# Attention gradient on one core: the queries for dK by copies and DMA transposes from SBUF instead of by a round trip through DRAM

## The chip, the cores and the metric

The kernel runs on one core of a Trainium2 chip. The metric is the device time in microseconds (us) of that core, the median over several executions. The engines of the core are TensorE (PE in the profile, its weight loads PEld), VectorE (DVE), ScalarE (ACT), GpSimd (POOL) and SyncE (SP), which only issues transfers. Transfers run on 16 DMA engines.

## The reference, cut to what matters

The program computes two blocks side by side, and for both the output and all gradients (out_0 to out_8). Block A is linear attention. Block B, in which the change lies, is attention with 16 query heads of 28 columns and one shared key and value head, over 2048 positions:

```python
q = (x @ wq).reshape(B, S, H, Dh).transpose(0, 2, 1, 3)   # H = 16, Dh = 28, S = 2048
k = x @ wk                                                # one head
v = x @ wv
scores = jnp.einsum("bhqd,bkd->bhqk", q, k) * (Dh ** -0.5)
p = softmax(scores)
o = jnp.einsum("bhqk,bkd->bhqd", p, v)
out = o.transpose(0, 2, 1, 3).reshape(B, S, H * Dh) @ wo
...
_out, _vjp = jax.vjp(f, A_x, A_wqkv, ..., B_wo)
_grads = _vjp(grad_out)
```

The gradient with respect to the scores, dS, is needed twice: dQ = dS k, and dK = dS^T q summed over all heads. dK is what the changed operand is for: its matmuls need q with query positions on the partitions.

## The kernel before, in words

Phase A (up to L527, about the first 195 us) does linear attention and its gradients. `phase_B_pre` (L529) projects x to q, k and v of block B. The queries lie in the tile R1, shape 128 x 4 x 2048: the partition is a column of a head (four heads of 32 rows each, 28 of them used), the second index is the group of four heads, the third is the query position. Row 0 of each 32 carries a shift that keeps the exponential in range. `q_shift` (L608) computes it for 512 positions, and `put_shift` (L615) writes it into R1 with four small transfers from GpSimd's queue.

The loop from L894 ("the core") runs over steps `u`, 512 of them and a tail of 28. Eight steps make a block `b`: one chunk of 256 query positions (`qc`, eight chunks), for one pair of heads (eight pairs). A step handles two tiles of 128 keys. The order of the work in the loop is written out by hand (`manual_schedule`), so each engine takes its instructions in the order in which the loop emits them. Work on one tile is spread over many steps:

- step u: TensorE forms scores (`rows_SD`, L668), ScalarE takes the exponential of both halves (L914, L964) into eT. After every fourth step SyncE transposes that group of eT to eN with a DMA transpose of 1 MB (L966).
- step u + 16: TensorE forms dP. VectorE multiplies one half by eT (L925). ScalarE copies the other half to cp (L927), and GpSimd multiplies it by eT (L928). The two products are dsT. The pool of dsT has five buffers, that of cp three.
- step u + 18: VectorE transposes dsT in squares of 32 to dsx (L995).
- from step u + 19: dQ (`dq_mm`); at odd steps dK (`dk_m`, L834), with dsx as one operand and qX as the other, first at u = 27. dV (`dv_mm`, L869) needs eN and the normalised output gradient don; the first at u = 20 needs the first two transposes of eT, the next at u = 28 the two after these.
- once a block: `o_norm` (L798) at steps with u mod 8 = 2, with three operations on GpSimd (prod L808, don L811, R L812); `row_D` (L814) at 4, with one on GpSimd (L817); then TensorE transposes don (L825) at 6. The queries of a finished block are overwritten with dQ (L949).
- in steps 1 to 25, odd ones, `do_proj` (L876) adds four matmuls of 512 columns and a copy on VectorE (L886).

qX for a chunk has the query positions of one partition group on its partitions, 32 for each a in 0 to 3, and for each position all 512 rows of heads. So the same q stands in four places, once for each row group of TensorE that `dk_m` uses. In the kernel before it is made so:

- for positions 0 to 1023, `phase_B_pre` transposes R1 with four DMA transposes (L598) into a tile that lies in gaT, and SyncE stores that as 1 MB in DRAM, the scratch qn_d (L599);
- for positions 1024 to 2047, four DMA transposes ahead of the loop (L893) write a tile qn that lies in one of the two qX buffers; GpSimd stores it in four parts in the steps 34, 42, 50 and 58 (L930);
- each qX is read from qn_d with four transfers of 256 KB from GpSimd's queue (L937): for chunk 0 in steps 10, 14, 18 and 22, for chunk 1 in 66 to 78, for chunk qc from 2 on in four steps of the 64 before, at u mod 64 = 34, 42, 50 and 58.

GpSimd also loads wo for the output projection in step 86 (L940). Transfers with GpSimd as issuer use queue 0, those of SyncE queue 1.

Of the kernel before, what the change touches and what calls it, by code (L numbers as in the profile page):

```python
# [11 lines left out]
BF16 = mybir.dt.bfloat16  # L12
# [13 lines left out]
def kernel(  # L26
# [40 lines left out]
    R2 = R2x[:, 1:NS + 1, :]  # L67
    R3 = reg.tile([P, 4, 1408], BF16, name="R3")
    R4 = reg.tile([P, 4, 512], BF16, name="R4")
    qn_d = dpool.tile([S, 512], BF16, name="qn_d")  # L70
    wqT_d = dpool.tile([512, D], BF16, name="wqT_d")
    wkvT_d = dpool.tile([64, D], BF16, name="wkvT_d")
    wo_d = dpool.tile([512, 512], BF16, name="wo_d")
# [51 lines left out]
    def phase_A(pa, cA, cB, awk, psA):  # L125
# [398 lines left out]
                nc.gpsimd.dma_start(wkvT_d[32 * w:32 * w + 32, 3 * P:D], wt[0:32, 4 * w + 3, 64:128])  # L524
        for q4 in range(4):
            dma_T(v4(R2), xa, 4 * q4, 4)
        return xbT, wq_pad, rep, bsel, gaB[:, 0:8, :], ga[:, 8:12, :], [flat(gaB[:, 2 * i + 8:2 * i + 10, :]).bitcast(F32) for i in range(3)]  # L527

    def phase_B_pre(pa, cA, awk, psA, io):  # L529
        xbT, wq_pad, rep, bsel, qn, sh, tmp = io  # L530
        kT, vT, vaug, kn, qT = kT_rep, vT_rep, vaug_, kn_, R1

        def gen(shape, dt=F32):
            return psA.tile(shape, dt, name="agen")

        ones16 = cA.tile([P, H], BF16, name="ones16")
        nc.gpsimd.memset(ones16[:], 1.0)
        nc.gpsimd.memset(ones16[0:1, :], 0.0)
        neg = cA.tile([P, 1], F32, name="neg")
        nc.gpsimd.memset(neg[:], 0.0)  # L540
        for j in range(4):
            nc.gpsimd.memset(neg[32 * j:32 * j + 1, :], -1.0)
        sel = cA.tile([P, 32], BF16, name="sel")
        nc.gpsimd.tensor_copy(out=sel[:], in_=identB[:, 0:32])
        nc.gpsimd.memset(sel[0:1, :], 0.0)
        kmx = cA.tile([H, NQC], F32, name="kmx")
        sqk = []
        def k_max(qc, sq):
            ps = gen([H, 512])
            mm(ps[:, :], ones16[0:32, :], sq[0:32, :])  # L550
            nc.vector.tensor_reduce(out=kmx[:, qc:qc + 1], in_=ps[:, :], axis=AX.X, op=ALU.max)

        prev = None
        for qc in range(NQC):
            for w, dst in [(0, kT), (1, vT)]:
                ps = gen([P, 512])
                for c in range(4):
                    mm(ps[:, :], rep[:, w, c, :], xbT[:, c, qc * 512:(qc + 1) * 512], start=(c == 0), stop=(c == 3))

                if w:  # L560
                    nc.vector.tensor_scalar(out=dst[:, qc * 512:(qc + 1) * 512], in0=ps[:, :], scalar1=neg[:, 0:1],
                                            scalar2=None, op0=ALU.add)
                else:
                    nc.scalar.activation(out=dst[:, qc * 512:(qc + 1) * 512], in_=ps[:, :], func=ACT.Identity,
                                         bias=neg[:, 0:1])
            sq = awk.tile([P, 512], BF16, name="osb")
            nc.vector.tensor_tensor(out=sq[0:32, :], in0=kT[0:32, qc * 512:(qc + 1) * 512],
                                    in1=kT[0:32, qc * 512:(qc + 1) * 512], op=ALU.mult)
            if prev is not None:
                k_max(qc - 1, prev)  # L570
            prev = sq
        shifts = [flat(sh)[0:H, i * 512:(i + 1) * 512] for i in range(2)] + [flat(R3)[r:r + H, 5120:5632] for r in (32, 0)]
        for qc in range(NQC):
            qs = slice(qc * 512, (qc + 1) * 512)
            pn = psA.tile([P, 512], F32, name="aacc")
            sqs = []
            for g in range(6):
                if qc == 0 and g == 2:
                    k_max(NQC - 1, prev)
                    nc.vector.tensor_reduce(out=kmax2[:], in_=kmx[:], axis=AX.X, op=ALU.max)  # L580
                if g < 4:
                    ps = gen([P, 512])
                    for c in range(4):
                        mm(ps[:, :], wq_pad[:, c, g * P:(g + 1) * P], xbT[:, c, qs], start=(c == 0), stop=(c == 3))
                    nc.scalar.activation(out=qT[:, g, qs], in_=ps[:, :], func=ACT.Copy)
                    sq = awk.tile([P, 512], BF16, name="osb")
                    nc.vector.tensor_tensor(out=sq[:, :], in0=qT[:, g, qs], in1=qT[:, g, qs], op=ALU.mult)
                    sqs.append(sq)
                if g >= 2:
                    mm(pn[:, :], bsel[:, g - 2, :], sqs[g - 2][:, :], start=(g == 2), stop=(g == 5))  # L590
            if qc == NQC - 1:
                break
            q_shift(pn, shifts[qc], tmp)
            if qc < 2:
                put_shift(shifts[qc], qs)
            if qc == 1:
                for g in range(4):
                    nc.sync.dma_start_transpose(qn[:, :, g * P:(g + 1) * P], qT[:, g, 0:1024])  # L598
                nc.sync.dma_start(qn_d[0:1024, :].rearrange("(t p) c -> p t c", p=P), qn)  # L599
        for rows, dst in [(vT, vaug_), (kT, kn_)]:  # L600
            ps = gen([P, NS, 32])
            for st in range(NS):
                mm(ps[:, st, :], rows[:, st * P:(st + 1) * P], sel[:, :])
            nc.vector.tensor_copy(out=dst, in_=ps[:])
        nc.gpsimd.memset(vaug_[:, :, 0:1], 1.0)
        return pn, shifts
# [5 lines left out]
        nc.vector.tensor_scalar(out=a.bitcast(i32), in0=a.bitcast(i32), scalar1=1, scalar2=None, op0=ALU.logical_shift_right)  # L612
        nc.vector.tensor_scalar(out=shift, in0=a, scalar1=1.004 * 2.0 ** 63.5, scalar2=None, op0=ALU.mult)

    def put_shift(shift, qs):  # L615
        for g in range(4):
            nc.gpsimd.dma_start(R1[:, g, qs].rearrange("(j r) s -> j r s", r=32)[:, 0, :], shift[4 * g:4 * g + 4, :])

    R3f = flat(R3)
    kT_rep, vT_rep = R3f[:, 0:2048], R3f[:, 2048:4096]  # L620
# [15 lines left out]
    with ExitStack() as cs_:  # L636
# [54 lines left out]

        woTp, gbT = R4, R2.rearrange("p t (c k) -> p t c k", k=P)

        identF = pp_.tile([P, P], F32, name="identF", bufs=1)
        make_identity(nc, identF[:])
        oTs = pp_.tile([P, 256], F32, name="oTs", bufs=1)
# [132 lines left out]
        def don_copy(b):  # L829
            r = 64 * (1 - b % 2)  # L830
            doT[b] = pw_.tile([P, 256], BF16, name="doT", bufs=2)
            nc.vector.tensor_copy(out=doT[b][r:r + 64, :], in_=tps2.pop(b)[r:r + 64, 0:256])

        def dk_m(b, m):  # L834
            qc, pair, g, hp = blk(b)
            h, B, s = m // 8, (m // 2) % 4, m % 2
# [51 lines left out]
        do_slots = {2 * i + 1: (i, 0, 512) for i in range(13)}  # L888
        do_slots.update({32 + 8 * n: (13 + n // 4, n % 4 * P, n % 4 * P + P) for n in range(12)})
        with tc.manual_schedule():  # L890
            qn = pqa_.tile([P, 8, 512], BF16, name="qX")
            for g in range(4):
                nc.sync.dma_start_transpose(qn[:, :, g * P:(g + 1) * P], R1[:, g, 1024:2048])  # L893
            for u in range(NU + 28):  # L894
                w = u - 16
                hasS = u < NU
# [18 lines left out]
                if u == 1:  # L915
                    q_shift(pn3, shifts[3], [pd_.tile([P, 2, 512], BF16, name="dsT").rearrange("p a b -> p (a b)").bitcast(F32)
                                             for _ in range(1)])
                    for qc in (2, 3):
                        put_shift(shifts[qc], slice(qc * 512, qc * 512 + 512))
                    dv_acc = psA.tile([P, 512], F32, name="aacc")  # L920
                if hasD:
                    dst = pd_.tile([P, 2, 512], BF16, name="dsT")
                    dsT[w] = dst
# [2 lines left out]
                    cp = pc_.tile([P, 512], BF16, name="cp")  # L926
                    nc.scalar.activation(out=cp[:, :], in_=dp[1][:, :], func=ACT.Copy)  # L927
                    nc.gpsimd.tensor_tensor(out=dst[:, 1, :], in0=cp[:, :], in1=ew[:, 1, :], op=ALU.mult)  # L928
                for n in {34: (0,), 42: (1,), 50: (2,), 58: (3,)}.get(u, ()):
                    nc.gpsimd.dma_start(qn_d[1024 + 256 * n:1280 + 256 * n, :].rearrange("(t p) c -> p t c", p=P),  # L930
                                        qn[:, 2 * n:2 * n + 2, :])
                for a in {10: (0,), 14: (2,), 18: (1,), 22: (3,), 66: (0,), 70: (2,), 74: (1,), 78: (3,)}.get(u, ()) or {
                        34: (0,), 42: (2,), 50: (1,), 58: (3,)}.get(u % 64, ()) * (96 < u < 448):
                    qc = u // 64 + (u > 96)
                    if a == 0:
                        qX[qc] = (pqa_ if qc % 2 else pqb_).tile([P, 4, 2, 512], BF16, name="qX")
                    nc.gpsimd.dma_start(qX[qc][32 * a:32 * a + 32, :, :, :].rearrange("j b s c -> j b (s c)"),  # L937
                                        qn_d[qc * 256:(qc + 1) * 256, :].rearrange("(b j s) c -> j b (s c)", b=4, s=2))
                if u == 86:
                    nc.gpsimd.dma_start(wo, wo_d[:, 0:D].rearrange("(g p) c -> p g c", p=P))  # L940
                if (b := due(u, 12)) is not None:
                    row_D(b)
                if u == 7:
# [19 lines left out]
                if hasS:  # L963
                    nc.scalar.activation(out=eT(u)[:, 1, :], in_=sp[1][:, :], func=ACT.Exp, scale=scale)  # L964
                    if u % 4 == 3:
                        nc.sync.dma_start_transpose(ENs[u // 4 % 6][:, :, :],  # L966
                                                    ETs[u // 4 % 5][:, :, :, :].rearrange("p a b c -> p (a b c)"))

                if u % 2:
                    b, i = divmod(u - 27, 8)  # L970
# [140 lines left out]
```

## Time and profile before

| what | value |
|---|---|
| time, median of 3 (lowest to highest) | 1080.88 us (1080.34 to 1081.75) |
| span of the profiled execution | 1080.6 us |
| busy: PE, DVE, ACT, POOL | 1026.0, 898.0, 873.2, 774.0 us |
| mean granted TensorE clock | 0.994 |
| products on GpSimd, L928 | 512, mean 1156 ns |
| eN transposes, L966 | 128, 1 MB each |
| qX reads, L937 | 32 of 256 KB, mean 582 ns on GpSimd |
| qn_d stores on GpSimd, L930 | 4 of 256 KB, mean 757 ns |
| TensorE's transposition of don waiting for GpSimd (L825 for L817) | 10.2 us in 29 waits |

The page of the profile divides the span into 40 slices of 27 us, with one digit for the busy share of each engine in tenths. Rows of an engine give the start, the duration, the operation with its tiles, and in brackets how long the engine stood idle before it and for whom. The chain of waits is followed backwards from the last instruction. In a row of a stretch the engines are in the order PE, PEld, DVE, ACT, POOL; then follow the granted clock, the DMA share and GB/s. SyncE's rows show how long the issue of a transfer held its queue.

### The profile page before, as it was taken

Reading aid. Unit: us, or ns where it says so; the run is one execution under the profiler, and the core shown is the slowest. Engines: PE = TensorE matmul, PEld = TensorE weight load, DVE = VectorE, ACT = ScalarE, POOL = GpSimd, SP = SyncE. Lnnn points to the kernel's source line nnn. Section 1 sums busy time; section 2 is a strip of 40 time slices with the busy share of each in tenths; the row PEclk is TensorE's granted clock in tenths of the full one; section 3 lists DMA queues with packets and bytes.
Section 4 is the critical chain, followed back from the end, with each engine's and each line's share of the span. In section 5 each row is a group of like instructions: output and inputs, shape, how many; then the busy total and the mean of one; then the engine's idle time right before and its main releaser. Section 6 shows DMA issues by size and latency. Waiting matters only on the chain.

```text
span 1080.6 us, 39970 instructions
## 1 busy us (share of the span) xinstructions
PE 1026.0 (95%) x16241; PEld 484.7 (45%) x16241; DVE 898.0 (83%) x1793; ACT 873.2 (81%) x1741; POOL 774.0 (72%) x1018
## 2 busy tenths in 40 slices
PE   9999999996999999999999999999999999999998
PEld 5555545432444444444444444444444444444434
DVE  7887400556999999999999999999999999999933
ACT  6463122585999999999999999999999999999622
POOL 6001242235899888888988988988988898888881
PEclk9999999997999999999999999999999999999999
DMA  9759899199999999999999999999999999999973
GB/s 265 160 110 199 173 204 228 30 185 151 204 208 211 203 202 188 200 180 210 179 185 197 196 195 187 203 181 188 185 209 187 196 198 162 206 187 181 223 133 90
DMA packets 668305, 199.34 MB, mean 184 GB/s; under 512 B 646056, under 2 KB 663760, under 8 KB 668120
## 3 DMA queue, kind: packets, MB, share of 16 engines
q1 hardware_dynamic: 655256, 174.18, 95.7%
q0 software_dynamic: 7904, 18.64, 6.8%
q10 hardware_dynamic: 4960, 3.96, 1.3%
q8 instruction: 127, 2.08, 0.8%
q14 instruction: 58, 0.48, 0.1%
HBM read 20.99 MB, written 12.94 MB: 31 GB/s over the span
## 4 chain that ended last, share of the span: by engine, by line
PE 37%; POOL 21%; ACT 18%; DVE 11%; issue 10%; DMA 4%; ACTq 0%; DVEq 0%; POOLq 0%
POOL dsT L928 16%; PE agen L82 14%; ACT cp L927 9%; ACT eT L964 7%; PE agen L661 7%; PE aacc L82 7%; PE aacc L661 6%; DVE dsx L995 4%; DVE dsT L925 2%; DMA eN<-eT 2%; POOL prod L808 2%; POOL don L811 1%; POOL R L812 1%; ACT eT L914 1%; DMA qX<-qn_d 1%
## 5 line engine op out<-in xcount | busy, mean ns | idle before, releaser
L928 POOL TENSOR_TENSOR dsT<-cp,eT 128x512 bf16<-128x512 bf16 x512 | 587.8, 1156 | 103.7 <-ACT cp L927 97.2
L995 DVE STREAM_TRANSPOSE dsx<-dsT 128x512 f32<-128x512 f32 x512 | 358.0, 699 | 2.8 <-POOL dsT L928 0.3
L925 DVE TENSOR_TENSOR dsT<-agen,eT 128x512 bf16<-128x512 f32 x512 | 342.1, 668 | 20.0 <-PE agen L661 15.2
L661 PEld LDWEIGHTS <-R 32*128 32x128 bf16 (+1 forms) x9104 | 225.3, 94 | 276.1 <-issue 239.5
L914 ACT ACTIVATE eT<-aacc 128x512 bf16<-128x512 f32 x512 | 313.2, 612 | 26.7 <-PE agen L661 15.8
L927 ACT ACTIVATE cp<-agen 128x512 bf16<-128x512 f32 x512 | 315.4, 616 | 12.3 <-PE agen L661 11.2
L964 ACT ACTIVATE eT<-aacc 128x512 bf16<-128x512 f32 x512 | 321.7, 628 | 0.0
L661 PE MATMUL agen<-dsx,qX 32*32 32x512 bf16 x4096 | 269.0, 376 | 3.5 <-DMA qX<-qn_d 3.5
L661 PE MATMUL agen<-doT,R 32*128 32x256 bf16 x2048 | 248.1, 270 | 3.3 <-DVE dsT L925 1.6
L661 PE MATMUL aacc<-R,R 32*128 32x256 bf16 (+1 forms) x2240 | 218.8, 269 | 5.8 <-DVE oTs L804 1.3
L661 PE MATMUL agen<-eT,R 128*32 128x256 bf16 x2048 | 158.2, 275 | 0.1
L661 PE MATMUL agen<-dsT,R 128*32 128x256 bf16 x2048 | 157.3, 275 | 0.1
L661 PEld LDWEIGHTS <-qX 32*32 32x32 bf16 x4096 | 80.1, 89 | 118.4 <-issue 54.6
L661 PE MATMUL aacc<-eN,don 128*32 128x512 bf16 x1024 | 98.1, 383 | 4.3 <-DMA eN<-eT 4.3
L82 PEld LDWEIGHTS <-R 128*128 128x128 bf16 (+1 forms) x517 | 41.0, 99 | 43.9 <-issue 12.3
L407 POOL COPY pk<-R 128x256 bf16<-128x256 bf16 x4 | 1.6, 397 | 73.8 <-DVE R L367 73.7
L82 PE MATMUL agen<-R,R 128*128 128x448 bf16 (+1 forms) x180 | 42.9, 366 | 0.5 <-ACT R L226 0.5
L661 PEld LDWEIGHTS <-don 128*32 128x32 bf16 x1024 | 33.9, 98 | 5.3 <-issue 4.7
L423 DVE TENSOR_TENSOR osb<-aacc,pr 64x448 bf16<-64x448 f32 x2 | 1.2, 617 | 39.1 <-DMA out_dram<-osb 24.9
L825 PE MATMUL aacc<-identB,don 128*32 128x128 bf16 x256 | 18.6, 224 | 14.0 <-POOL don L817 10.2
L949 DVE TENSOR_SCALAR R<-agen 64x256 bf16<-64x256 f32 x64 | 27.3, 427 | 3.6 <-PE agen L661 1.6
L517 ACT ACTIVATE wdq<-agen 128x448 bf16<-128x448 f32 x16 | 8.7, 543 | 24.7 <-PE agen L82 24.7
(232 smaller groups left out, 987.7 us busy)
## 6 DMA issues: line engine op xcount, KB each, us to landing
qX<-qn_d POOLq DMA_DIRECT2D x32, 256.0 KB, 4.4
out_dram<-osb ACTq DMA_DIRECT2D x22, 112.0 KB
eN<-eT SPq DMA_TRANSPOSE x128
xa<-in_A_x_dram SPq DMA_DIRECT2D x8, 224.0 KB
ga<-in_grad_out_dram SPq DMA_DIRECT2D x4, 448.0 KB
xa<-in_grad_out_dram POOLq DMA_DIRECT2D x4, 448.0 KB, 5.8
out_dram<-wdq POOLq DMA_DIRECT2D x8, 224.0 KB, 4.9
eT<-in_grad_out_dram SPq DMA_DIRECT2D x4, 448.0 KB
```

The costliest lines, as they stand in the source:

```text
L82: nc.tensor.matmul(out_ap, lhsT=lhsT, rhs=rhs, start=start, stop=stop, tile_position=(0, 0))
L661: nc.tensor.matmul(out, lhsT=lhsT, rhs=rhs, start=start, stop=stop, tile_position=pos, skip_group_check=True)
L808: nc.gpsimd.tensor_tensor(out=prod[b][:], in0=dnv, in1=os_, op=ALU.mult)
L811: nc.gpsimd.tensor_tensor(out=dn[:], in0=dnv, in1=r_[:].to_broadcast([P, 2, 2, 32]), op=ALU.mult)
L825: nc.tensor.transpose(tp2[q:q + 32, qb * P:(qb + 1) * P], don[b][:, qb, h, :], identB[:, :], tile_position=(0, q))
L914: nc.scalar.activation(out=eT(u)[:, 0, :], in_=sp[0][:, :], func=ACT.Exp, scale=scale)
L925: nc.vector.tensor_tensor(out=dst[:, 0, :], in0=dp[0][:, :], in1=ew[:, 0, :], op=ALU.mult)
L927: nc.scalar.activation(out=cp[:, :], in_=dp[1][:, :], func=ACT.Copy)
L928: nc.gpsimd.tensor_tensor(out=dst[:, 1, :], in0=cp[:, :], in1=ew[:, 1, :], op=ALU.mult)
L949: nc.vector.tensor_scalar(out=qT_B[g][64 * hp:64 * hp + 64, qc * 256:(qc + 1) * 256], in0=oq[64:128, 0:256], scalar1=scale, scalar2=None, ...
L964: nc.scalar.activation(out=eT(u)[:, 1, :], in_=sp[1][:, :], func=ACT.Exp, scale=scale)
L995: nc.vector.transpose(out=dsx[b][:, tp, :, :, :].rearrange("p h t c -> p (h t c)").bitcast(F32), in_=dsT[y][:, :, :].rearrange("p h c -> p ...
```

## The change

q for dK no longer goes through DRAM. For one chunk and one group of four heads, two copies (`qc_copy`, one for even and one for odd positions) read 256 positions of R1 with a step of two elements and write each of them four times into a staging tile of 128 x 1024 elements. One DMA transpose (`qc_T`) then writes these to qX. The four DMA transposes L598, the four L893, both stores to qn_d, the reads of qX and qn_d itself go.

- Chunk 0 is made ahead of the loop: four copies on GpSimd, four on VectorE, in four buffers of dsT, and four DMA transposes.
- Chunks 1 to 7 are made in the 64 steps before: GpSimd's two copies in the steps u mod 64 = 30 and 31 for group 0, 38 and 39 for group 1, and so on, behind the product of the step, in the staging tile qst, which has one buffer. The transpose is issued right behind the eN transpose of the second step.
- wo is loaded by SyncE ahead of the loop.
- `put_shift` for the positions from 1024 on moves from GpSimd's queue in step 1 to SyncE's queue in step 11.
- Chunk 0's qX uses the buffer that qn had; even and odd chunks change places.

The instructions of TensorE and ScalarE and their order stay the same.

```diff
-            if qc == 1:
-                for g in range(4):
-                    nc.sync.dma_start_transpose(qn[:, :, g * P:(g + 1) * P], qT[:, g, 0:1024])
-                nc.sync.dma_start(qn_d[0:1024, :].rearrange("(t p) c -> p t c", p=P), qn)
...
+        qst = pp_.tile([P, 8, 4, 32], BF16, name="qst", bufs=1)[:, :, :, :]
...
+        def qc_copy(eng, st, qc, g, s):
+            src = qT_B[g][:, qc * 256:(qc + 1) * 256].rearrange("p (b j s) -> p b j s", b=4, s=2)[:, :, :, s]
+            eng.tensor_copy(out=st.rearrange("p (b s) a j -> p b s a j", s=2)[:, :, s, :, :],
+                            in_=src.unsqueeze(2).to_broadcast([P, 4, 4, 32]))
+
+        def qc_T(st, qc, g):
+            nc.sync.dma_start_transpose(qX[qc].rearrange("p b s c -> p (b s) c")[:, :, g * P:(g + 1) * P],
+                                        st.rearrange("p n a j -> p (n a j)"))
...
-            qn = pqa_.tile([P, 8, 512], BF16, name="qX")
+            nc.sync.dma_start(wo, wo_d[:, 0:D].rearrange("(g p) c -> p g c", p=P))
+            qX[0] = pqa_.tile([P, 4, 2, 512], BF16, name="qX")
             for g in range(4):
-                nc.sync.dma_start_transpose(qn[:, :, g * P:(g + 1) * P], R1[:, g, 1024:2048])
+                st = pd_.tile([P, 2, 512], BF16, name="dsT").rearrange(
...
+                qc_copy(nc.gpsimd, st, 0, g, 0)
+                qc_copy(nc.vector, st, 0, g, 1)
+                qc_T(st, 0, g)
...
-                    for qc in (2, 3):
-                        put_shift(shifts[qc], slice(qc * 512, qc * 512 + 512))
+                if u == 11:
+                    for n in (2, 3):
+                        put_shift(nc.sync, shifts[n], slice(n * 512, n * 512 + 512))
...
-                for n in {34: (0,), 42: (1,), 50: (2,), 58: (3,)}.get(u, ()):
-                    nc.gpsimd.dma_start(qn_d[1024 + 256 * n:1280 + 256 * n, :].rearrange("(t p) c -> p t c", p=P),
-                                        qn[:, 2 * n:2 * n + 2, :])
-                for a in {10: (0,), 14: (2,), 18: (1,), 22: (3,), 66: (0,), 70: (2,), 74: (1,), 78: (3,)}.get(u, ()) or {
-                        34: (0,), 42: (2,), 50: (1,), 58: (3,)}.get(u % 64, ()) * (96 < u < 448):
...
-                    nc.gpsimd.dma_start(qX[qc][32 * a:32 * a + 32, :, :, :].rearrange("j b s c -> j b (s c)"),
-                                        qn_d[qc * 256:(qc + 1) * 256, :].rearrange("(b j s) c -> j b (s c)", b=4, s=2))
-                if u == 86:
-                    nc.gpsimd.dma_start(wo, wo_d[:, 0:D].rearrange("(g p) c -> p g c", p=P))
+                gq, iq = divmod(u % 64 - 30, 8)
+                qq = u // 64 + 1
+                if 0 <= gq < 4 and u < 448:
+                    if gq == 0 and iq == 0:
+                        qX[qq] = (pqb_ if qq % 2 else pqa_).tile([P, 4, 2, 512], BF16, name="qX")
+                    if iq < 2:
+                        qc_copy(nc.gpsimd, qst, qq, gq, iq)
...
                         nc.sync.dma_start_transpose(ENs[u // 4 % 6][:, :, :],
                                                     ETs[u // 4 % 5][:, :, :, :].rearrange("p a b c -> p (a b c)"))
+                    if 0 <= gq < 4 and iq == 1 and u < 448:
+                        qc_T(qst, qq, gq)
```

## The prediction

> **What bounds the kernel now.** I read the slices of the page first, then the chain of waits, then stretches of one loop block (eight steps of `u`, L946 to the next L946) and the rows of the engines in them.
>
> ```profile
> PE   9999999996999999999999999999999999999998
> ...
> PEclk9999999997999999999999999999999999999999
> ```
>
> TensorE is over 90% busy in every slice but the tenth (243 to 270 us), and there its clock falls too. The chain of waits names two transfers around that slice:
>
> ```profile
> 232.62 16.89 DMA eN<-eT
> ...
> 255.79 10.60 DMA qX<-qn_d
> ```
>
> In TensorE's rows they are real stops, with the wait in brackets:
>
> ```profile
> 249.56 1.04 PE L661 MATMUL aacc<-eN,don 128*32 128x512 bf16 x6 [4.35 <-DMA eN<-eT]
> ...
> 266.44 1.88 PE L661 MATMUL agen<-dsx,qX 32*32 32x512 bf16 x13 [3.49 <-DMA qX<-qn_d]
> ```
>
> The stretches show what the two blocks cost: length, busy time by engine, granted clock.
>
> ```profile
> 240.36:259.53 19.17, 13.62 (x156) 5.24 (x154) 13.00 (x25) 12.38 (x25) 11.65 (x15) 0.82 1.28 154
> 259.53:277.86 18.33, 13.73 (x230) 5.78 (x230) 12.63 (x26) 12.05 (x25) 10.23 (x12) 0.81 1.24 175
> 277.86:290.22 12.36, 11.64 (x236) 5.30 (x230) 11.91 (x24) 12.07 (x25) 11.02 (x14) 1.00 1.21 211
> ...
> 412.02:424.18 12.16, 11.48 (x220) 5.06 (x214) 11.61 (x23) 11.97 (x25) 10.83 (x14) 1.00 1.15 199
> 424.18:436.22 12.04, 11.62 (x219) 5.20 (x214) 11.59 (x23) 11.97 (x25) 10.36 (x13) 1.00 1.05 181
> ```
>
> So the loop has two regimes. Two early blocks take 37.50 us, where a block otherwise takes 12. In all others ScalarE (11.97 of 12.04), VectorE and TensorE are nearly full, and GpSimd has some 1.7 us left. Blocks with a read of qX on GpSimd take 12.16 (12.36 with a store to qn_d), the others 11.96 to 12.04. Why GpSimd matters though it isn't full:
>
> ```profile
> 415.12 0.57 POOL L937 DMA_DIRECT2D qX<-qn_d  x1
> 415.70 0.44 POOL L808 TENSOR_TENSOR prod<-R,oTs 128x128 f32<-128x128 bf16 x1
> ...
> 419.04 0.22 POOL L817 TENSOR_TENSOR don<-Dq,rl 128x4 bf16<-128x4 f32 x1
> ```
>
> The issue stands directly ahead of prod, don and L817, and TensorE's transposition of don (L825) waits for L817: 10.2 us in 29 waits.
>
> Why eN is late is in SyncE's rows, its transposes in order:
>
> ```profile
> 226.62 5.95 SPq L966 DMA_TRANSPOSE eN<-eT  x1
> 232.62 8.96 SPq L966 DMA_TRANSPOSE eN<-eT  x1
> 241.62 12.27 SPq L966 DMA_TRANSPOSE eN<-eT  x1
> ```
>
> The first waits behind the q transposes (L598, L893) and goes 3.5 us after its eT was done at 223.1. The second and third take 9 and 12 us instead of the usual 4.9 to 6.1, while the store of qn_d and the reads of qX run.
>
> **What the Trainium skill says.** "TensorE: Matmul & The Clock Gate", section "What's actually happening": the clock halves after an idle window of about 3.4 us and returns after one busy window. The trace agrees: mean clock 0.82 and 0.81 in the two blocks with stops of 4.35 and 3.49 us, 1.00 elsewhere. "DMA: Bandwidth & Descriptors", section "Issuing engines are not separate DMA queues": transfers of all issuers interleave on the same 16 DMA engines. The 8.96 and 12.27 above fit that. "GPSIMD Engine Reference", section "3.1 Elementwise — side-by-side cycle accounting": about 1.03 cycles per element with one input, 2.6 with two. The trace: copies of 256 and 448 elements take 397 and 561 ns (0.854 ns each), the two-input product of 512 takes 1156. Section "7. Performance pitfalls for Q7 kernels" puts a surcharge on reads with a step over 8 bytes; the new copy steps 4 bytes. No run here shows a strided read.
>
> **The change, part by part.**
>
> *Start.* Removed: four transposes L598 (5.5 us of SyncE), the 1 MB store of qn_d, four L893 (1.23 + 2.22 + 2.29 + 1.57 us) and four qX reads; all of it stood ahead of eN or beside it. Added on SyncE: wo's load (taken as 0.4, like the store L599 at 0.36), four transposes from staging (1.36 each; the unhindered L598 took 1.24 to 1.39). Their sources are four copies each on GpSimd and VectorE. VectorE waited 2.06 us for L610 at 220.76, which hides most of its four; I take 0.6 each, 2.4 in all, so 0.4 us of delay, with VectorE waiting over 1 us in nearly every pair of the next steps. Copies run from about 218.3, the transposes end near 225.2, so the first eN leaves about 1.4 us earlier and the second ends near 236 instead of 241.6, with no DRAM traffic beside it. It is wanted at 245 and qX[0] near 256. Both stops should go. Without them these steps ran at 1.70 us (254.23 to 262.71, five starts of L925), because of do_proj. Eight steps from u = 17 then take 13.6, the next block 3 x 1.70 + 5 x 1.5 = 12.6. Together 26.2, against 37.50: **-11.3 us**.
>
> *put_shift to SyncE at u = 11.* Eight small DMAs at about 0.5 us (SyncE's L1059 took 0.50), 4 us. Queued behind them are the third eN and those after it. By the ledger at 5.35 per eN, the third leaves near 240 and the fourth lands near 253, wanted at u = 28, near 257. Hidden, with 4 us to spare.
>
> *Reads and stores of qX, removed from GpSimd.* Chunks 2 to 7 had 24 blocks at 12.16 with one issue each; at the other blocks' mean of about 12.02 (12.04, 11.96, 12.13, 11.96) that is 24 x 0.14 = 3.4. Four blocks with L930, 12.35 to 12.02: 1.3. The two with double issues for chunk 1, 0.15 each: 0.3. Together **-5.0 us**. wo's issue was hidden.
>
> *qc_copy on GpSimd.* 56 copies, two in each of 28 blocks, in units 6 and 7. Line through the two copies above: 561 + 64 x 0.854 = 616 ns; taken as 0.62. The nearest dearer row is the two-input 1.156, the upper end. A block without qX reads holds 10.36, plus 1.24 is 11.60 of 12.0. By order: GpSimd has caught up by unit 6 (it waits 0.31 us for cp ahead of each product from 432.34 on). A unit is 1.47 long and a product takes 1.12 start to start when queued, so unit 7 starts 0.26 late, unit 0 0.53, unit 1 0.18, unit 2 on time. Queued behind the copies are only the products; VectorE's transposition of them comes two steps later, and cp has three buffers, so this lag is hidden. At 0.9 us a copy unit 2 would be some 0.4 late, which is 0.17 less than the issue that goes. Cost **0**, up to 0.65 us a block at 1.156 (10.36 + 2.31 = 12.67 against 12.02).
>
> *Transposes of qst, 28 on SyncE.* 2 x 5.3 + 1.36 + gaps of 0.1 is 12.2 in a block of 12.0; eN now leaves 0.03 us after its eT, and its reader comes 13 steps (19 us) later, so a lag of under 1 us over four blocks is hidden. But qst has one buffer: the next group's copy, seven steps on, waits until the transposition has landed. It ends about 7 us after the eT of its unit and lands within some 2 us; the copy comes near 11.2. In the first chunk SyncE is still about 5 us behind, so I add **+1.0 us** for waits there, between 0 and 3.
>
> Sum: 1080.9 - 11.3 - 5.0 + 1.0 = 1065.6; I say **1065.5**.
>
> **The rivals.**
>
> A. SyncE takes the stop's place: wo, the shifts and the staged transposes push eN 5 us further back, and half of the stop returns at u = 20 or 28, with half the clock's loss. For it: SyncE is some 15 us behind at 260 as it is. Against: each item removed there was dearer than the one added. 5 of the 11.3 lost: 1070.5.
>
> B. GpSimd becomes the bound: the copies cost like two-input products, 1.156, and 28 blocks stretch to 12.67. Start -11.3, remaining gains of four blocks none, 28 x (12.67 - 12.16) = +14.3, waits +1: 1085, slower. For it: GpSimd is the only engine that receives work in every chunk. Against: all copies in the trace lie near 0.6.
>
> C. One buffer of qst: the copies wait for the landing in all seven chunks, about 1 us in three of four groups, half of it passed on to don: 21 x 0.5 = 10: less the 1.0 counted, 1074.5.
>
> D. More than I count: the block at 895.85 to 909.61 took 13.76, and GpSimd waited 1.3 us ahead of its L937 there. If that wait came from that issue, and the waits of the first chunk don't appear: 1063.
>
> **How the numbers follow.** Forecast 0.56, D 0.12, A 0.14, C 0.11, B 0.07. D lies inside the bounds of the start's estimate (a block of 12.0 instead of 13.6 takes it to about 1061). A is inside the range and C half a microsecond beyond its edge, B is left out. Range 1059 to 1074. Faster by over 0.2%, that is below 1078.7: 0.93 (all but B); same 0.01; slower 0.06.
>
> **What would show it.** Right: in the tenth slice PE at 9 and a clock of 9; no waits for eN or qX; the two blocks from u = 17 near 13.6 and 12.6 us; eN issues at 4.9 to 5.5 throughout; qst copies of 0.6 us; blocks of 12.0 in all chunks. Wrong: waits of GpSimd for a DMA ahead of qst (C), copies near 1.1 us with GpSimd's waits for cp gone (B), TensorE waiting for eN with put_shift just ahead of it on SyncE (A). The steps I am least sure of are the copy's price and the landing of the small transposes.

## The result, and the profile after

The changed kernel takes 1066.06 us (median of 4 runs, 1065.49 to 1068.99), the kernel before 1081.32 us on the same chip. The ratio is 0.9849, with a 95% interval of 0.9801 to 0.9898. All ratios leave out runs over 1.5% above the fastest of the same kernel; only the kernel before and x3 have such runs. Taken again later, five runs gave 1067.54 us and a ratio of 0.9883 (0.9846 to 0.9921). The forecast was 1065.5.

In the slices of the changed kernel's page, the tenth slice rises from 6 to 8 for TensorE and from 7 to 9 for its clock:

```profile
PE   9999999998999999999999999999999999999998
...
PEclk9999999999999999999999999999999999999999
```

The stretches shown are the two blocks from u = 17, a block of the first chunk, and a later block (length; busy PE, PEld, DVE, ACT, POOL; clock, DMA share, GB/s):

```profile
240.37:253.82 13.45, 11.50 (x156) 5.07 (x154) 12.82 (x26) 12.28 (x25) 10.57 (x13) 1.00 1.13 169
253.82:266.40 12.58, 11.50 (x232) 5.63 (x230) 12.39 (x26) 11.79 (x25) 10.90 (x14) 1.00 1.14 208
278.44:291.72 13.28, 11.61 (x238) 5.36 (x230) 12.03 (x25) 12.01 (x25) 13.22 (x17) 1.00 1.14 207
...
424.20:436.20 12.00, 11.65 (x234) 5.57 (x234) 11.57 (x24) 11.93 (x25) 10.36 (x13) 1.00 1.21 198
```

The clock is full, 13.45 and 12.58 stand where 19.17 and 18.33 stood, and one block of 13.28 is new. SyncE's queue at the start, repeated rows joined (x2 is two transposes):

```profile
217.89 0.36 SPq L896 DMA_DIRECT2D wo<-wo_d  x1
219.78 5.37 SPq L836 DMA_TRANSPOSE qX<-dsT  x4
225.21 10.52 SPq L972 DMA_TRANSPOSE eN<-eT  x2
235.77 4.54 SPq L612 DMA_DIRECT2D R<-R  x8
240.40 20.98 SPq L972 DMA_TRANSPOSE eN<-eT  x4
```

The first eN leaves at 225.21, the second ends at 235.7, and each of those shown takes 4.9 to 5.5 us. GpSimd's rows show what made the block of 13.28:

```profile
274.54 1.15 POOL L939 TENSOR_TENSOR dsT<-cp,eT 128x512 bf16<-128x512 bf16 x1 [0.31 <-ACT cp L938]
277.66 0.61 POOL L832 COPY qst<-R 128x512 bf16<-128x512 bf16 x1 [1.97 <-DMA qX<-qst]
```

The copy for group 1 waits until the transposition of group 0 has emptied qst. The products behind it start late, and TensorE meets the delay in the next block. There are four such waits in the loop (1.97, 0.67, 0.21, 1.08), in its group of the page:

```profile
L832 POOL COPY qst<-R 128x512 bf16<-128x512 bf16 x56 | 34.2, 611 | 4.0 <-DMA qX<-qst 3.9
```

The chain of waits, by engine, is now TensorE's and ScalarE's; GpSimd's share falls from 21% to 5% (before, then after):

```profile
PE 37%; POOL 21%; ACT 18%; DVE 11%; issue 10%; DMA 4%; ACTq 0%; DVEq 0%; POOLq 0%
PE 43%; ACT 32%; issue 14%; POOL 5%; DVE 4%; DMA 1%; ACTq 0%; DVEq 0%; POOLq 0%
```

Where the time went, between the starts of the block marker (L946 before, L952 after); "forecast" is the prediction's terms put to the stretches:

| stretch | before | after | difference | forecast |
|---|---|---|---|---|
| up to u = 17 | 240.36 | 240.36 | 0 | 0 |
| u = 17 to 33 | 37.50 | 26.03 | -11.47 | -11.3 |
| u = 33 to 65 | 49.38 | 49.73 | +0.35 | -0.3 |
| u = 65 to 97 | 48.32 | 48.27 | -0.05 | -0.3 |
| chunks 2 to 7, u = 97 to 481 | 582.97 | 579.20 | -3.77 | -3.4 |
| u = 481 to 513 | 48.74 | 49.00 | +0.26 | 0 |
| rest | 73.29 | 72.14 | -1.15 | 0 |

The last row isn't explained by the change: over the runs below it lies between 71.7 and 73.3.

### The profile page after: what moved, and what is told of

Read it like the earlier page. It is cut to its first block, busy times and chain, and to the rows that moved or that the text cites. A ratio compares the mean times of both kernels' runs of the same rounds, so it can differ in the third digit from the quotient of the medians.

```text
span 1064.7 us, 40036 instructions
## 1 busy us (share of the span) xinstructions
PE 1023.1 (96%) x16241; PEld 489.1 (46%) x16241; DVE 899.5 (84%) x1797; ACT 870.4 (82%) x1741; POOL 780.7 (73%) x1033
## 4 chain that ended last, share of the span: by engine, by line
PE 43%; ACT 32%; issue 14%; POOL 5%; DVE 4%; DMA 1%; ACTq 0%; DVEq 0%; POOLq 0%
ACT cp L938 16%; PE agen L81 14%; ACT eT L970 13%; PE agen L656 10%; PE aacc L656 10%; PE aacc L81 5%; POOL dsT L939 3%; PE aacc L790 2%; ACT eT L924 2%; PE aacc L821 1%; DVE dsT L936 1%; DVE dsx L1003 1%; DMA out_dram<-dsT 1%; POOL eT L754 1%; POOL out_dram L778 0%
## 5 line engine op out<-in xcount | busy, mean ns | idle before, releaser
L939 POOL TENSOR_TENSOR dsT<-cp,eT 128x512 bf16<-128x512 bf16 x512 | 587.9, 1156 | 78.9 <-ACT cp L938 71.7
L656 PEld LDWEIGHTS <-R 32*128 32x128 bf16 (+1 forms) x9104 | 227.9, 94 | 274.1 <-issue 238.4
L832 POOL COPY qst<-R 128x512 bf16<-128x512 bf16 x56 | 34.2, 611 | 4.0 <-DMA qX<-qst 3.9
L804 POOL TENSOR_TENSOR prod<-R,oTs 128x128 f32<-128x128 bf16 x64 | 27.6, 431 | 9.3 <-DVE oTs L800 9.3
```

The source lines that it names most:

```text
L656: nc.tensor.matmul(out, lhsT=lhsT, rhs=rhs, start=start, stop=stop, tile_position=pos, skip_group_check=True)
L804: nc.gpsimd.tensor_tensor(out=prod[b][:], in0=dnv, in1=os_, op=ALU.mult)
L832: eng.tensor_copy(out=st.rearrange("p (b s) a j -> p b s a j", s=2)[:, :, s, :, :], in_=src.unsqueeze(2).to_broadcast([P, 4, 4, 32]))
```

## The experiments

Theory: the start's gain comes from SyncE's queue ahead of eN and the traffic beside it; the loop's gain from the DMA issues that leave GpSimd; the copies cost nothing because of where they stand. The rivals are written with each run. Ratios are to the kernel before, whose median over all its runs was 1081.88, 1081.69 and 1079.98 us in the three groups of runs (x, y, z). Each group ran on another chip; the changed kernel ran again beside the z group alone (z4), so where an x or y run is set against it, the stretches of the traces decide. What is left out of an edit is marked by three dots.

### x1: every copy twice

```diff
+                        for _ in range(2):
                             qc_copy(nc.gpsimd, qst, qq, gq, iq)
```

> The changed kernel with every copy of the loop (L832, 56 of them on GpSimd) done twice into the same qst. Theory: one pair of copies (1.22 us) is hidden by the 1.6 us that GpSimd has free in a block of 12.0 us, a second pair isn't: 10.36 + 2.44 = 12.8 us of work, so the 28 copy blocks go from 12.0 to about 12.7 and the kernel from 1066 to about 1085 (ratio to the kernel before about 1.004). Rival: GpSimd is not near the bound even then, since three cp buffers and the two steps until dsT is transposed take up the lag: under +4 us, 1066 to 1070. Second rival: already the first pair costs 0.3 us a block, then the doubled pair costs 28 x 1.2 = 34 us, 1100.

Measured: 1084.78 us, ratio 1.0042 (1.0023 to 1.006). A block with copies and one without:

```profile
378.12:390.75 12.63, 11.60 (x236) 5.32 (x230) 11.96 (x25) 12.02 (x25) 12.44 (x17) 1.00 1.01 191
428.01:439.97 11.96, 11.61 (x236) 5.51 (x230) 11.77 (x25) 11.89 (x25) 10.32 (x13) 1.00 1.20 197
```

GpSimd, at 12.44 of 12.63, is now the bound. Most copy blocks take 12.6 us instead of 12.0, a few 13.2 and more. The first pair lay within the slack and the second one passes it, as the theory said.

### x2: the copies four steps earlier

```diff
-                gq, iq = divmod(u % 64 - 30, 8)
+                gq, iq = divmod(u % 64 - 26, 8)
```

> The changed kernel with the copies four steps earlier, in units 2 and 3 of a block, so that the first stands directly ahead of prod, don and L813, where the DMA issue of qX stood before. Theory: place decides; a copy of 0.61 us there holds up don as the issue of 0.57 us did, TensorE waits again at L821 for L813, 28 x 0.15 = +4 us: 1070 (ratio 0.990). Rival: only GpSimd's total load counts, it is the same: 1066 (ratio 0.985).

Measured: 1086.69 us, ratio 1.0055 (1.0034 to 1.0076); 27 of the 28 copy blocks take 12.69 instead of 12.03 (one of them 12.91, one 17.17 with a wait of 2.59 for qst in it; the first block, beside do_proj, stays at 12.59). That is +20.6 us against the changed kernel, five times what was expected, and slower than the kernel before. GpSimd's rows:

```profile
374.25 0.61 POOL L832 COPY qst<-R 128x512 bf16<-128x512 bf16 x1
374.82 0.43 POOL L804 TENSOR_TENSOR prod<-R,oTs 128x128 f32<-128x128 bf16 x1
...
377.02 0.61 POOL L832 COPY qst<-R 128x512 bf16<-128x512 bf16 x1
377.59 1.16 POOL L939 TENSOR_TENSOR dsT<-cp,eT 128x512 bf16<-128x512 bf16 x1
378.70 0.23 POOL L813 TENSOR_TENSOR don<-Dq,rl 128x4 bf16<-128x4 f32 x1
```

My expectation counted only the first copy. Both stand ahead of L813: 1.22 us where the issue put 0.57. The issue cost a block 0.14, so by estimate 0.43 of such a delay is hidden; 1.22 - 0.43 = 0.79 is near the measured 0.66. The load is the same as in the changed kernel; the place alone makes 20 us, some 15 by what stands ahead of L813 and some 5 in the block with the wait for qst.

### x3: the reads of qX issued by SyncE, in the kernel before

```diff
-                    nc.gpsimd.dma_start(qX[qc][32 * a:32 * a + 32, :, :, :]...
+                    (nc.sync if u > 96 else nc.gpsimd).dma_start(qX[qc][32 * a:32 * a + 32, :, :, :]...
```

> The kernel before with one edit: the 24 reads of qX for chunks 2 to 7 (L937) are issued by SyncE instead of GpSimd; data, traffic and landing stay. Theory: the issue on GpSimd, 0.57 us ahead of prod and don, is what made these blocks 12.16 instead of 12.02: 24 x 0.14 = -3.4 us, 1078 (ratio 0.997). Rival: the reads themselves (their traffic beside eN) stretch the blocks: no change, 1081 (ratio 1.000). Second rival: SyncE's issues push eN back and TensorE waits for it: slower than 1081.

Measured: 1073.24 us, ratio 0.9936 (0.9912 to 0.996). In the trace chunks 2 to 7 take 578.06 instead of 582.97 us: -4.91. Of it 24 x 0.14 = 3.4 is as expected. Another 1.57 is the block at 895.85 of the kernel before, 13.76 us with GpSimd's wait ahead of its read, which takes 12.19 here: the issue on GpSimd caused that block too. The same traffic still runs, so it isn't the traffic. The profiled span is 7.15 us shorter than that of the kernel before; the other 2.2 us lie where the edit does nothing (ahead of the loop, in the start's stops, behind the loop). GpSimd's row of that read in the kernel before:

```profile
900.30 0.59 POOL L937 DMA_DIRECT2D qX<-qn_d  x1 [1.30 <-issue]
```

The groups of the transposition of don, in the order: kernel before, x3, the changed kernel, x2, x1 (the number behind the name of GpSimd's small product, L817 or L813, is the time that TensorE stood idle for it):

```profile
L825 PE MATMUL aacc<-identB,don 128*32 128x128 bf16 x256 | 18.6, 224 | 14.0 <-POOL don L817 10.2
```

```profile
L825 PE MATMUL aacc<-identB,don 128*32 128x128 bf16 x256 | 18.6, 222 | 8.8 <-POOL don L817 2.5
```

```profile
L821 PE MATMUL aacc<-identB,don 128*32 128x128 bf16 x256 | 18.5, 221 | 8.4 <-POOL don L813 1.6
```

```profile
L821 PE MATMUL aacc<-identB,don 128*32 128x128 bf16 x256 | 18.6, 223 | 27.2 <-POOL don L813 22.7 <-ACT eT L924 0.6
```

```profile
L821 PE MATMUL aacc<-identB,don 128*32 128x128 bf16 x256 | 18.6, 223 | 25.1 <-POOL don L813 20.4 <-ACT eT L924 0.6
```

10.2, 2.5, 1.6, 22.7, 20.4: in all five this one wait follows what stands ahead of L813 (L817) in GpSimd's queue, in x1 the products held up by the doubled copies, and the length of chunks 2 to 7 follows it (583.0, 578.1, 579.2, 593.7, 596.1 us), if not in exact order.

### x4: a second buffer for qst in chunks 0 and 1

```diff
+        qsts = [qst, flat(wo)[:, 0:1024].rearrange("p (n a j) -> p n a j", n=8, a=4)]
...
-            nc.sync.dma_start(wo, wo_d[:, 0:D].rearrange("(g p) c -> p g c", p=P))
...
-                        qc_copy(nc.gpsimd, qst, qq, gq, iq)
+                        qc_copy(nc.gpsimd, qsts[gq % 2 if u < 128 else 0], qq, gq, iq)
...
```

> The changed kernel with a second buffer for qst in chunks 0 and 1 (u < 128), in the space of wo, whose load moves from the start to u = 127. Theory: the waits of GpSimd ahead of the copies in chunk 0 (1.97 and 0.67 us) are what made these blocks 13.28 and 12.38 us; with two buffers they go, the blocks take 12.0 to 12.1 and the kernel 1064.5 (1.6 us less). Rival: those blocks are long because SyncE is behind with eN or because of do_proj beside them, and GpSimd's wait is only a sign of it: the waits go and the blocks stay, 1066.

Measured: 1065.8 us (1064.32 to 1068.34), ratio 0.9872 (0.9834 to 0.991). The waits of the first chunk are gone and its blocks, u = 33 to 65, take 47.98 instead of 49.73 us, so the single buffer costs 1.75 us there. The block of 13.28 becomes:

```profile
278.40:290.40 12.00, 11.62 (x238) 5.58 (x230) 11.81 (x25) 11.93 (x25) 11.35 (x15) 1.00 1.26 183
```

In the time it can't be told from the changed kernel: at u = 174 and 182 copies waited 1.36 and 0.43 us for the buffer, which is single there.

### y1: the L893 transposes late, in the kernel before

```diff
-            for g in range(4):
-                nc.sync.dma_start_transpose(qn[:, :, g * P:(g + 1) * P], R1[:, g, 1024:2048])
...
-                for n in {34: (0,), 42: (1,), 50: (2,), 58: (3,)}.get(u, ()):
+                for n in {50: (0,), 54: (1,), 58: (2,), 62: (3,)}.get(u, ()):
...
+                    if u in (35, 39, 43, 47):
+                        g = (u - 35) // 4
+                        nc.sync.dma_start_transpose(qn[:, :, g * P:(g + 1) * P], R1[:, g, 1024:2048])
```

> The kernel before with one edit: the four transposes of q at L893 (7.3 us of SyncE) stand behind the eN transposes of u = 35, 39, 43 and 47 instead of ahead of the first one, and the stores L930 follow at u = 50 to 62. The store of qn_d, the qX reads and their traffic stay at the start. Theory A: SyncE's queue decided the start: the first eN leaves at 223.1 instead of 226.6, the second ends near 238 instead of 241.6, the 4.35 us stop goes and with it the fourth qX read comes earlier, so most of the second stop: the two blocks from u = 17 take about 30 us instead of 37.5, the kernel about 1074. Theory B: the DRAM traffic decided it: the second and third eN still take 9 and 12 us, the stops move but stay, the two blocks take 35 to 37.5 and the kernel 1079 to 1081.

Measured: 1079.15 us, ratio 0.999 (0.9966 to 1.0014). The time seems to speak for B; the trace says otherwise. SyncE's queue:

```profile
220.93 0.36 SPq L599 DMA_DIRECT2D qn_d<-gaT  x1
223.16 40.91 SPq L964 DMA_TRANSPOSE eN<-eT  x7
```

The first eN leaves at 223.16, and seven take 40.9 us, 5.8 each with gaps, beside the whole store and all four reads. The two blocks from u = 17 take 26.03 us, not the 30 of theory A but the full gain of 11.47. Most of it was lost again at the edit's other end, where the store of the same qn (L930, now L928) waits for the late transposes, with prod and don queued behind it:

```profile
301.23 0.78 POOL L928 DMA_DIRECT2D qn_d<-qX  x1 [7.67 <-DMA qX<-R]
```

That block takes 21.66 us. So 7.3 us less in SyncE's queue removes both stops of the start, with the traffic in place.

### y2: the traffic alone put back

```diff
...
+            nc.sync.dma_start(qn_d[0:1024, :].rearrange("(t p) c -> p t c", p=P), flat(R1)[:, 0:4096]...
...
+                for a in {10: (0,), 14: (2,), 18: (1,), 22: (3,)}.get(u, ()):
...
+                    nc.gpsimd.dma_start(xd[32 * a:32 * a + 32, :, :, :]..., qn_d[0:256, :]...
```

> The changed kernel with the DRAM traffic of the start put back and nothing else: one 1 MB store to qn_d by SyncE behind the four staged transposes, and four reads of 256 rows by GpSimd at u = 10, 14, 18, 22 into the tile that is not yet in use; nobody waits for what they bring. Theory B (traffic): the second and third eN take 9 and 12 us again instead of 5, SyncE is 8 to 10 us later, the fourth eN lands near 262 and TensorE stops for about 5 us, with its clock halved after it: +5 to +8 us, 1071 to 1074. Theory A (queue order alone): eN stays under 6.5 us each, no stop, under +1 us.

Measured: 1072.89 us, ratio 0.9932 (0.9898 to 0.9966). The size is that of theory B; the place is another. The first two eN take 7.75 and 6.92 us instead of 5.50 and 4.97, and SyncE runs 12.6 us behind eT at the fourth (8.3 in the changed kernel). Still the two blocks from u = 17 take 26.17: no stop for eN. SyncE is still 8.6 us late at u = 31, and there the single qst turns it into a wait:

```profile
281.87 0.61 POOL L833 COPY qst<-R 128x512 bf16<-128x512 bf16 x1 [6.49 <-DMA qX<-qst]
```

```profile
278.11:297.52 19.41, 14.46 (x236) 5.82 (x230) 12.26 (x24) 12.34 (x25) 14.14 (x18) 0.74 1.14 205
```

The copy of u = 38 holds up the products behind it, and the clock falls to 0.74. This one block costs 7.4 us over a block of 12.04. It is 6.1 us longer than the same block of the changed kernel (13.28), which has a wait there too, and makes most of the 7.4 us by which the span is longer (1072.1 against 1064.7).

### y3: the queue work alone put back

```diff
+            qd = pqb_.tile([P, 4, 2, 512], BF16, name="qX").rearrange("p b s c -> p (b s) c")
+            for g in range(4):
+                nc.sync.dma_start_transpose(qd[:, :, g * P:(g + 1) * P], R1[:, g, 1024:2048])
```

> The changed kernel with SyncE work of the kernel before put back and no DRAM traffic: four transposes of 256 KB like L893, behind the four staged ones, into the tile that is not yet in use; nobody waits for them. Theory A (queue): they hold SyncE for 5.5 to 7.3 us, the first eN leaves near 231 to 232, the fourth lands near 257 to 259, wanted near 256: a stop of 1 to 3 us, +1 to +4 us. Theory B (traffic alone matters): no stop, under +0.5 us.

Measured: 1073.06 us, ratio 0.992 (0.989 to 0.995). The first eN leaves at 231.15, six us later than in the changed kernel, and the two blocks still take 26.03 us, which theory A did not expect:

```profile
239.78:265.81 26.03, 22.91 (x383) 10.68 (x384) 25.21 (x50) 24.07 (x49) 21.50 (x27) 1.00 0.97 163
```

Then the same wait as in y2: 6.37 us ahead of the copy at 281.49, a block of 19.35.

### y4: put_shift spread over u = 64 to 92

```diff
...
-                if u == 11:
-                    for n in (2, 3):
-                        put_shift(nc.sync, shifts[n], slice(n * 512, n * 512 + 512))
+                if 64 <= u < 96 and u % 4 == 0:
+                    n, g = divmod((u - 64) // 4, 4)
+                    put_shift(nc.sync, shifts[n + 2], slice(n * 512 + 1024, n * 512 + 1536), (g,))
```

> The changed kernel with the eight DMAs of put_shift spread over u = 64 to 92, one in four steps, instead of all eight on SyncE at u = 11. Theory: they are hidden by 4 us of room as they stand, so the start doesn't change; SyncE has 4 us less of delay in chunk 0, so the waits for the single qst buffer there (1.97 and 0.67 us) go: -1 to -1.6 us, 1064.5 to 1065. Rival: the eight DMAs cost TensorE something at the start after all: -2 us or more. Second rival: nothing changes.

Measured: 1071.85 us, ratio 0.991 (0.9875 to 0.9944): slower than the changed kernel, which no theory had. The start is unchanged (26.03), and u = 33 to 65 falls from 49.73 to 48.23, so the expected 1.5 us came. But the first copy of chunk 2 reads the tile R1 that put_shift writes, in other columns, and the program lets it wait for the last of the eight:

```profile
366.91 0.61 POOL L832 COPY qst<-R 128x512 bf16<-128x512 bf16 x1 [6.75 <-DMA R<-R]
```

A block of 18.47 us, +6.4, is the price.

### z1: the kernel before, reordered, with its way through DRAM

```diff
-            for g in range(4):
-                nc.sync.dma_start_transpose(qn[:, :, g * P:(g + 1) * P], R1[:, g, 1024:2048])
...
-                for n in {34: (0,), 42: (1,), 50: (2,), 58: (3,)}.get(u, ()):
-                    nc.gpsimd.dma_start(qn_d[1024 + 256 * n:1280 + 256 * n, :]...
+                for n in {46: (0,), 50: (1,), 54: (2,), 58: (3,)}.get(u, ()):
+                    nc.sync.dma_start(qn_d[1024 + 256 * n:1280 + 256 * n, :]...
...
-                    nc.gpsimd.dma_start(qX[qc][32 * a:32 * a + 32, :, :, :]...
+                    (nc.sync if u > 24 else nc.gpsimd).dma_start(qX[qc][32 * a:32 * a + 32, :, :, :]...
...
+                    if u in (27, 31, 35, 39):
+                        g = (u - 27) // 4
+                        nc.sync.dma_start_transpose(qn[:, :, g * P:(g + 1) * P], R1[:, g, 1024:2048])
```

> The kernel before, its way through DRAM kept, with the order alone changed: the four L893 transposes stand behind the eN transposes of u = 27, 31, 35, 39, and SyncE instead of GpSimd issues the stores L930 (now at u = 46, 50, 54, 58) and the qX reads of chunks 1 to 7. Theory: what the change brings is the order of SyncE's queue at the start and GpSimd's freedom from issues, not the copies nor the missing DRAM traffic. Then the two blocks from u = 17 take 26.0 us (-11.5), chunks 2 to 7 lose 4.9 us as with the reads alone moved, the four L930 blocks take 12.0 instead of 12.35 (-1.3): 1081.5 - 17.7 = 1063.8, ratio 0.984. Rival: the traffic costs too, so eN takes longer and a stop of several us comes back somewhere in the first 100 steps: 1070 or more, ratio over 0.989.

Measured: 1065.47 us (1063.52 to 1067.68), ratio 0.9868 (0.983 to 0.9905); the changed kernel beside it 1067.54. The two blocks from u = 17:

```profile
240.36:253.80 13.44, 11.50 (x156) 5.07 (x154) 12.88 (x26) 12.27 (x25) 11.58 (x15) 1.00 1.18 215
253.80:266.38 12.58, 11.51 (x231) 5.65 (x230) 12.39 (x26) 11.79 (x25) 10.24 (x12) 1.00 1.21 185
```

Chunks 2 to 7 take 579.34 us, as in the changed kernel (579.20), where 578.06 was expected (x3); u = 33 to 65 takes 48.80, with one block of 12.86 that I can't explain. Without a copy and with all DRAM traffic, the gain is the same within what the measurement can tell.

### z2: both start loads put back, with two qst buffers in chunks 0 and 1

The edits of y2, y3 (ahead of the staged transposes) and x4 together.

> The changed kernel with both start loads put back, the four transposes of 256 KB (ahead of the staged ones) and the 1 MB store with four reads of 256 rows, and with a second qst buffer in chunks 0 and 1 so that GpSimd's copies don't wait. Each load alone left the two blocks from u = 17 at 26.0 to 26.2 us and came out as one wait of 6 to 7 us for the single qst. Theory: at the start the two loads together pass the room: first eN near 231, eN of 7 to 9 us, fourth landing 262 to 266 against 257: a stop of 5 to 9 us comes back there, the two blocks take 31 to 36 us and the kernel 1071 to 1077. Rival: the single buffer is the only place where SyncE's backlog costs anything, and with two buffers none of it is seen: 26 us and 1064 to 1066.

Measured: 1075.03 us, ratio 0.9962 (0.9943 to 0.9981). The time is in the expected range, its parts are not. At the start the second eN is late by one wait:

```profile
248.10 0.61 PE L657 MATMUL aacc<-eN,don 128*32 128x512 bf16 x6 [1.19 <-DMA eN<-eT]
```

and the two blocks take 14.5 and 13.4, 27.9 us together: 1.9 of the 5 to 10 expected. With two buffers the first chunk has no wait for qst, although SyncE is some 10 us behind. The backlog lives on until qst is single again; the block with the copy of u = 166:

```profile
476.78:494.54 17.76, 14.22 (x234) 5.65 (x230) 12.34 (x24) 12.18 (x25) 14.65 (x19) 0.81 1.23 192
```

A wait of 5.08 us ahead of one copy there costs 5.8. So the two loads together do pass the room at the start, but by little, and they don't rebuild the stops that made 37.5 us of the two blocks.

### z3: x4 and put_shift at u = 64 to 76; z4: the changed kernel again

```diff
...
+                if 64 <= u < 80 and u % 4 == 0:
+                    n, g = divmod((u - 64) // 2, 4)
+                    put_shift(nc.sync, shifts[n + 2], slice(n * 512 + 1024, n * 512 + 1536), (g, g + 1))
```

> The changed kernel with the second qst buffer in chunks 0 and 1 and put_shift spread over u = 64 to 76, two DMAs in four steps, so that all have landed well before the first copy of chunk 2 (u = 94). Theory: no waits for qst in chunk 0 and none for put_shift, blocks of 12.0 there: 1.7 us less than the changed kernel, 1064.3. Rival: the spread of the later blocks (single ones of 12.4 to 12.7 without a wait that repeats) is as large as that, so no difference to be seen: 1066.

> The changed kernel as it is, beside the three others on the same chip, to compare with them: 1066.

Measured: z3 1068.42 us (1064.99 to 1072.38), ratio 0.9897; z4 1067.54, ratio 0.9883. No gain. Chunk 0 takes 47.98 as expected and chunk 2 has no wait, but SyncE now reaches the output transposition at u = 130 four us late, is 7.4 us behind after it and still 3.7 at u = 159; the copies at u = 166, 174 and 302 wait 1.4 to 2.4 us. The backlog was moved, not removed.

## Why the prediction was right

- **Start, -11.3:** measured -11.47, with 13.45 and 12.58 against 13.6 and 12.6, and the first two eN at the times given. The prediction named queue and traffic together. The runs part them: moving L893 is enough with the traffic kept (y1, z1), and either load put back alone leaves TensorE without a stop at the start (y2, y3). So it is shown what removes the stops, but only in part what made them: with both loads back (z2) the first two eN take 7.79 and 6.72 us, where the second and third of the kernel before took 8.96 and 12.27, and the stops are small. In the kernel before three of the four L893 transposes stood behind the store, in z2 all four stand ahead of it; that order was not tried, nor was the kernel before without its traffic alone.
- **put_shift hidden:** at the start yes (26.03 with and without, y4). But its 4 us stay in SyncE's queue and come out in chunk 0 as waits for qst: 1.5 us.
- **Issues off GpSimd, -5.0:** x3 confirms the 24 reads by themselves: 3.4. For the four stores, u = 33 to 65 takes 47.98 in x4, where no copy waits, against 49.38 before: 1.4 where 1.3 was counted.
- **Copies at 0.62, cost 0:** 611 ns, and hidden (x1, x2). The Trainium skill, "GPSIMD Engine Reference", section "7. Performance pitfalls for Q7 kernels", puts its surcharge on steps over 8 bytes; this read with a step of 4 bytes took the 616 ns of the line through two copies within 1%.
- **Waits for qst, +1.0:** this term was too small, if inside its bounds of 0 to 3. The waits sum to 3.9 us and cost about 2.2: 1.75 in chunk 0 (x4) and 0.4 to 0.6 in the block of 12.61 with the wait of 1.08 (without a wait it takes 12.04 before and 12.25 in x4). SyncE was less behind than assumed (2.6 us at u = 31, not 5), but the buffer came free 3.3 to 5.1 us after the start of the issue (here at 277.66 for an issue at 272.59; in y3 at 281.49 for one at 278.18).
- **What made up for it:** the block of 13.76, which I had left to rival D. It is worth 1.57, and x3 shows that the read's issue caused it. A further block of 12.70 at 400.40 in the changed kernel has no wait that explains it. That the sum came within 0.6 us of the measured time is therefore luck in part: these two misses offset each other, 1.15 us of the difference in span lie behind the loop, where nothing was forecast, and single runs of the kernel before differ by more than 10 us.
- **The rivals:** A didn't happen, no instruction of TensorE in the core waits for eN. B is real with twice the copies, not with one pair. C happened in four places of 27, all where SyncE was 1.4 to 2.7 us behind eT; in z4, the same program, the two of the first chunk come again (1.85 and 0.75) and the later ones stand elsewhere (0.28 to 0.86).
- **The signs and a reading:** TensorE's tenth slice reads 8, not the 9 forecast, eN takes 4.8 to 6.8 us over the whole loop, not 4.9 to 5.5, and not all blocks take 12.0. In the kernel before, the last slice of TensorE also reads under 9, not the tenth alone; nothing rests on it.

## What to carry to other kernels

Look at what stands ahead of the small operation that another engine waits for, before counting an engine's load: here two copies of 0.6 us per block on GpSimd cost nothing in one place and some 15 us over the kernel in another. A queue that is nearly full pays a backlog back slowly, and it charges for it at the first buffer that has only one copy, often far from the cause; so ask for each moved transfer who is next in that queue and which wait will show it. Before replacing a round trip through DRAM, try to reorder it: here the order alone gave the whole gain, as far as the runs can tell (z1).

## What the runs showed of the hardware

- SyncE's backlog shrinks by some 0.5 us per eN transposition: from 7.4 us at u = 131 to 3.7 at u = 159 in z3, seven transpositions later. In the first chunk, where blocks have qst's transposition, it doesn't shrink: in x4 it grows from 2.9 us at u = 31 to 4.9 at u = 55.
- A short wait of GpSimd costs less than itself, a long one more: 1.08 cost 0.4 to 0.6 and 1.97 cost 1.24 at full clock; 5.08 cost 5.8 at a clock of 0.81, and 6.49 cost 7.4 at 0.74.
- What the clock adds can be seen in z2, where the wait of 5.08 us stopped TensorE for 2.35 us. In the 3.41 us up to 481.04 TensorE is busy for 0.94 us, and then its clock is halved for 6.83 us (rows of stretches, clock third from the end):

```profile
477.63:481.04 3.41, 0.94 (x22) 0.57 (x22) 0.16 (x1) 0.74 (x3) 1.92 (x3) 1.00 0.95 187
481.04:487.87 6.83, 6.00 (x73) 1.80 (x65) 5.41 (x11) 4.07 (x8) 6.74 (x10) 0.50 1.15 215
```

- In all these traces, the first 50 us and the end of the kernel apart, the clock is halved 13 times, for 3.41, 6.83 or 10.24 us, and in the 3.41 us before each TensorE was busy for 26 to 64%. No threshold can be read from this: some stretches of 55 to 65% weren't followed by a halved clock. The Trainium skill, "TensorE: Matmul & The Clock Gate", section "What's actually happening", names an idle window of about 3.4 us. The prediction found the stops of 4.35 and 3.49 us in agreement with it; but there the clock was halved 2.5 and 1.8 us after they began (at 247.70 and 264.76), and shorter stops were enough too, 2.35 us in z2, 1.53 in x2 (halved at 276.74) and 1.19 in x1 (at 683.39).
- The start's stops seem to spread the time too. The kernel before ran between 1069.6 and 1097.6 us in 101 later runs (one more, of 2962.3, is left out), and x3, which keeps its start, between 1064.8 and 1081.1. Over the runs that the ratios use, the standard deviation is 3.5 to 4.0 us by group for the kernel before and 4.2 for x3; for all other kernels it is 0.8 to 2.6. The mean clock goes with the time: the three runs of the kernel before at 1.000 took 1069.6 to 1071.3 us, the 22 at 0.992 took 1081.3 to 1086.5. That the stops are the reason is inferred from this and from which kernels keep them; only one run of each was profiled.
